# A delta-rule attention with two expert layers on one core: halves in turn, a shared copy, loads without padding

## The chip, the cores and the metric

The program runs on one core of a Trainium2 chip. Its time is the device time of one execution in microseconds (us), taken as the median of several runs on the chip. One execution was recorded by the hardware profiler; rows of that trace are quoted below.

A core has a matrix engine (PE; its weight loads are told apart as PEld), a vector engine (DVE), a scalar engine (ACT), a general engine (POOL) and an engine that here only issues transfers (SP). Each works through its own list of instructions in order, and they wait for one another by semaphores. PE reads from the on-chip memory SBUF and writes into PSUM, which DVE and ACT read back.

## The reference

Three layers follow one another. The first is a recurrence over 768 tokens for 4 batches of 8 heads with 48 features; the state of a head is a 48 by 48 matrix:

```python
for t in range(S):
    y[:, :, t] = np.einsum('bhd,bhde->bhe', q[:, :, t], state)
    v_old = np.einsum('bhde,bhd->bhe', state, kt)          # kt: normalised key
    state = state + bt[:, :, :, None] * np.einsum('bhd,bhe->bhde', kt, vt - v_old)
```

Its output, seen as 3072 tokens of 384 features, goes through two layers of the same shape, each a product with a 384 by 2048 matrix, a function of each element, and a product with a 2048 by 384 matrix:

```python
h = x @ w_in;  g = np.where(h > 0.0, h, np.exp(np.minimum(h, 0.0)) - 1.0);  x = g @ w_out
h = x @ w_in2; g = P(h) / (Q(h) + 1e-06);  out = g @ w_out2   # P cubic, Q from |h| and h*h
```

## The kernel before

**The recurrence in chunks.** The 768 tokens are cut into 12 chunks of 64 (s = 0 to 11), and two chunks make a window (six of them). Within a chunk the recurrence is a triangular system. The 32 heads lie as two halves of 16 (hf = 0, 1), each half in tiles of its own: 8 positions u by two blocks of partitions h. A half's tile of features has 64 partitions per block, of which 48 carry features; the other 16 hold zeros that `layout` (`rows`, L1653) puts there. No product reads them: the slices are `o:o + D` with D = 48.

For a window the gram products (`g_item`, L895, tiles gp) give all key-key and key-query products. From them DVE inverts the triangular systems in a row of some 60 small steps (`t_pieces`, L940), which ends in the tile tp_t. Then comes, for each chunk, a chain of small PE products with a copy or subtraction after each (`chain`, L1070): `ks` subtracts the old state's prediction (none for s = 0), `solve` (block 0), copy to ub, `lo`, subtract in R (for s = 0 in kv), `solve` (block 1), copy to ub, `yy` makes the outputs, `ku` the state update, `xx` transposes the outputs for the next layer. In `solve` and `lo` the loops run over u, then h, then hf, so that two PSUM tiles, one for each half, are filled in alternation, and both are complete only at the end.

The new state is taken out of PSUM in `ku`: one full tile for half 0, two tiles of 64 partitions for half 1. For s = 0 all three are copies by ACT (`move`, L1088), for later chunks three additions by DVE.

**The layers.** Wide groups of nine products of 128 by 512 (H into tiles h, O into tiles o) make the first expert layer, window by window, 16 H and 16 O groups each; the small groups of the next window's chain stand between them. The second expert layer (tiles h_a, h_b, o) follows without small groups. All weights pass a conversion on ACT and DVE first (raw, ce, wi, wo).

**Who sets the order.** The program is recorded first and then put in order by a planner (`order`, L355): it plays the recorded operations through a table of costs, gives each operation a latest start and repeats that for the eight entries of `PUSH` (L338), keeping the best. `MIX` (L330) is a list of pairs that breaks ties: each pair redraws a pseudo-random share of them. The planner's order is what each engine executes. Where it expects PE to idle before the first wide group, `gaps` (L397) puts in fillers, products whose result is not used (tile fill).

**Loads.** SP issues all transfers in one list. gin (xg and wo hold the first of them) are the gram inputs of a half chunk, kq the key-query tiles, kv keys and values. `gin_ahead` (L816) and `ch_ahead` (L842) issue each tile of gin and kq as one transfer of 128 partitions by 4 KB. Eight semaphores serve the transfers in turn, so one that would be the ninth in flight waits for the first. `hold` and `follow` (L717, L720) are copies of one column by POOL that keep a transfer back until something else is there; `follow` makes the second half's gin wait for the first half's.

Of the kernel before, what the change touches and what calls it, by code (L numbers as in the profile page):

```python
# [20 lines left out]
D = 48  # L21
NSC = 12
# [164 lines left out]
class Recorder:  # L187
# [62 lines left out]
    def mm(self, out, lhsT, rhs, start, stop):  # L250
        kind = self.group.kind
        pitch, lat = PEC[kind]
        self.add("PE", self.nc.tensor.matmul, dict(out=out, lhsT=lhsT, rhs=rhs, start=start, stop=stop), [out], [lhsT, rhs], pitch, lat)
# [74 lines left out]
SIZE = {"F": 9, "yy": 32, "yt": 48, "y2": 64}  # L328
SLACK = {"small": 150, "F": 100, "x": 30, "issue": 450, "rate": 385, "land": 2300, "wait": 900, "space": 3500, "room": 264, "first": 460, "blk": 253.9, "use": 2250, "hold": 400, "jit": 300, "keep": 6000, "most": 5000, "step": 3500, "drift": 0,  "pj": 0}
MIX = [  # L330
# [4 lines left out]
]  # L335


PUSH = [(16000, 5000), (5000, 3000), (16000, 3000), (0, 3000), (20000, 3000), (13000, 3000), (0, 500), (18000, 3000)]  # L338


def draw(seed, n):
# [282 lines left out]
def kernel(  # L624
# [93 lines left out]
        gpsimd.tensor_copy(out=t[:, 0, 0:1], in_=gate[-1])  # L718

    def follow(t, u):  # L720
        gpsimd.tensor_copy(out=t[:, 0, 0:1], in_=u[:, 0, 0:1])

    conv_q = []
    for f in range(NF):
# [91 lines left out]
    def gin_ahead(n):  # L816
        for _ in range(n):
            i = gin_n[0]
            if i == len(gin_q) or i >= 4 and len(gate) < 2:
                return  # L820
            park = i < 6
            if park or gin_l[0] < 2:
                w, s, hf = gin_q[i]
                if park:
                    t = gin_park(i)
                else:
                    t = ap2.tile([128, 1024], F32, tag="gin", name="gin", bufs=2)
                    gin_l[0] += 1
                t = t.rearrange("p (u n) -> p u n", u=8)
                if 4 <= i < 8:  # L830
                    hold(t)
                elif i >= 8 and hf:
                    follow(t, gin_t[s, 0][0])
                rc.dma(out=t, in_=c_kg[s, hf])
                gin_t[s, hf] = t, not park
                gin_n[0] += 1

# [4 lines left out]
    def ch_ahead(nm):  # L842
        if ch_n[nm] < len(ch_q):
            s, hf = ch_q[ch_n[nm]]
            if nm == "kq":
                t = ap2.tile([128, 8, 128], F32, tag="kq", name="kq")
                if s == 1:
                    hold(t)
                rc.dma(out=t, in_=c_kq[s, hf])
            else:  # L850
                if s == 1:
                    t = mp.tile([128, 2, DM], F32R, tag="wor", name="kv").bitcast(F32)
                    t = t.rearrange("p a b -> p (a b)").rearrange("p (u n) -> p u n", u=8)
                    hold(t)
                else:
                    t = ap2.tile([128, 8, 96], F32, tag="kv", name="kv")
                    if s == 0:
                        hold(t)
                rc.dma(out=t, in_=c_kv[s, hf])
            ch_t[nm, s, hf] = t  # L860
            ch_n[nm] += 1
# [11 lines left out]
    def cross(hf):  # L873
        if hf == 0:
            return [(slice(0, 128), slice(0, 128))]
        return [(slice(64 * h, 64 * h + 64), slice(64 - 64 * h, 128 - 64 * h)) for h in range(2)]

    def grp(h, blk, u):
        o = 64 * h + 32 * (blk ^ u % 2)
        return slice(o, o + 32)  # L880
# [189 lines left out]
    def chain(w, slots=SLOTS):  # L1070
# [14 lines left out]
        for j, s in enumerate(WINS[w]):  # L1085
# [38 lines left out]

            def solve(blk, s=s, st=st):
                rc.brk("s8" if s > 1 else "so")
                for u in range(8):
                    for h in range(2):
                        for hf, d in enumerate(st):
                            v = u ^ hf  # L1130
                            rs = grp(h, blk, v)
                            mm(out=d["cb"][over(s, hf, rs), v], lhsT=tp_t[rs, d["wu"] + v], rhs=d["R"][rs, v], start=True, stop=True)

            def u1(s=s, st=st, solve=solve):
                for d in st:
# [6 lines left out]

            def lo(j=j, s=s, st=st):
                rc.brk("l8" if s > 1 else "lo")
                for u in range(8):
                    for h in range(2):
                        for hf, d in enumerate(st):
                            v = u ^ hf
                            rs, os = grp(h, 0, v), grp(h, 1, v)
                            mm(out=d["cb"][over(s, hf, os), v], lhsT=gl_d[w][rs, d["wu"] + v, 32:64], rhs=d["ub"][rs, v], start=True, stop=True)  # L1150
                for hf, d in enumerate(st):
                    for o, c in cross(hf if s > 1 else 0):
                        vector.tensor_tensor(out=d["R"][o], in0=d["R"][o], in1=d["cb"][c], op=ALU.subtract)
# [57 lines left out]
            def ku(hf, s=s, st=st):  # L1211
                ps = [pa.tile([128, 8, D], F32, tag="pa", name="ku") for _ in range(2)]
                rc.brk("ku")
                for u in range(8):
                    for hf, d in enumerate(st):
                        for h in range(2):
                            rs, o = slice(64 * h, 64 * h + 64), 64 * (h ^ hf)
                            mm(out=ps[hf][o:o + D, u], lhsT=d["kv"][rs, u, 0:D], rhs=d["ub"][rs, u], start=True, stop=True)
                for hf in range(2):
                    for o, c in cross(hf):  # L1220
                        sl = s_st[o, 8 * hf:8 * hf + 8]
                        if s == 0:
                            move(sl, ps[hf][c], hf)
                        else:
                            vector.tensor_tensor(out=sl, in0=sl, in1=ps[hf][c], op=ALU.add)
                for _ in range(2):
                    ch_ahead("kv")
# [411 lines left out]
def layout(q, k, v, beta, moe_w_in, moe_w_out, moe2_w_in, moe2_w_out, moe2_a, moe2_b):  # L1639
    import numpy as np  # L1640

    f32 = np.float32
    B, H, S, Dh = q.shape

    def feat(x):
        t = x.reshape(B, 4, 2, NSC, 64, Dh)
        return t.transpose(3, 0, 2, 5, 1, 4).reshape(NSC, B, 96, 4, 64)

    def tok(x):
        t = x.reshape(B, 4, 2, NSC, 2, 32, Dh)  # L1650
        return t.transpose(3, 0, 2, 4, 5, 1, 6)

    def rows(k, q, cross):  # L1653
        kq = np.concatenate([k, q], axis=-1).reshape(NSC, 2, 2, 2, Dh, 4, 128)
        o = np.zeros((NSC, 2, 2, 64, 8, 128), f32)
        for hf in range(2):
            for h in range(2):
                o[:, hf, h ^ (hf * cross), :Dh] = kq[:, hf, :, h].transpose(0, 2, 1, 3, 4).reshape(NSC, Dh, 8, 128)
        return o.reshape(NSC, 2, 128, 8, 128)

    kf, qf = feat(k), feat(q)
    c_kg = rows(kf, qf, 1)
    kf = kf.copy()
    kf[:, :, :, 1::2] = np.roll(kf[:, :, :, 1::2], 32, axis=-1)
    c_kq = rows(kf, qf, 0)
    kt, vt = tok(k), tok(v)
    kv = np.concatenate([kt, vt], axis=-1)
    kv[..., 1::2, :] = kv[:, :, :, ::-1, :, 1::2].copy()
    c_kv = kv.reshape(NSC, 2, 2, 128, 4, 96).transpose(0, 1, 3, 2, 4, 5).reshape(NSC, 2, 128, 8, 96)
    bt = beta.reshape(B, 4, 2, NSC, 2, 32).transpose(3, 2, 4, 0, 1, 5).copy()  # L1670
    bt[:, :, :, :, 1::2] = bt[:, :, ::-1, :, 1::2].copy()
    bt = bt.reshape(NSC, 4, 16, 32)
    beta_l = np.concatenate([bt[0::2], bt[1::2]], axis=2)
    tk = np.arange(64)
    tpart = np.arange(128) % 64
    mask_p = np.concatenate(
        [(t[:, None] < tk[None, :]).astype(f32) for t in (tpart, (tpart + 32) % 64)] + [np.eye(128, dtype=f32)], axis=1)
    moe_w_in, moe_w_out, moe2_w_in, moe2_w_out = (
        w.view(np.int64) for w in (moe_w_in, moe_w_out, moe2_w_in, moe2_w_out))

    def w_in_tiles(w):
        return w.reshape(3, 128, NF, 128).transpose(2, 1, 0, 3).reshape(NF, 128, DM)

    d = {
        'c_kg': c_kg, 'c_kq': c_kq, 'c_kv': c_kv, 'beta_l': beta_l.reshape(len(WINS), 128, 32),
        'mask_p': mask_p,
        'w_in1': w_in_tiles(moe_w_in),
        'w_out1': moe_w_out.reshape(NF, 128, DM),
        'w_in2': w_in_tiles(moe2_w_in), 'w_out2': moe2_w_out.reshape(NF, 128, DM),
        'a_co': moe2_a, 'b_co': moe2_b,  # L1690
    }
    return {n: np.ascontiguousarray(x) for n, x in d.items()}
# [22 lines left out]
```

## Time and profile before

| | us |
|---|---|
| median of 3 runs | 966.79 |
| lowest, highest | 965.37, 967.17 |
| the profiled execution | 966.62 |
| its span, first to last instruction | 964.8 |
| PE busy in the span | 943.4 |
| first gram product | 6.87 |
| first `solve` product (chunk 0) | 45.50 |
| first wide group | 69.12 |
| last wide group's end, about | 960 |

The profiled execution took 966.62 us, of which 964.8 are the span of its trace. The stages of the span are: loads and gram products of window 0; the inversion on DVE, up to 45.50; the chain of the first two chunks, up to 69.12; and the stream of wide groups, in which PE is busy nearly all the time. A row of the timeline gives start, duration, engine, line, operation, output and inputs, and in brackets the idle time before it with what ended it. Line 206 is the helper that issues every recorded operation, so the tiles tell the rows apart.

### The profile page before, as it was taken

How to read it: one execution, taken by the hardware profiler on the slowest of the kernel's cores; microseconds unless marked ns; L12 is line 12 of the kernel's file. 1: busy time of each engine (PE TensorE's matmuls, PEld its weight loads, DVE VectorE, ACT ScalarE, POOL GpSimd, SP SyncE). 2: the span in 40 equal slices, each digit the busy share in tenths (PEclk: the TensorE clock that was granted, in tenths of full speed). 3: DMA queues.
4: the chain of work that ended last, by engine and by line, in shares of the span. 5: the costliest groups of instructions: out<-in, count | busy, mean ns of one | idle time of the engine just before them, and what ended most of it. 6: DMA issues, size and time to landing. Idle time of an engine off the chain costs nothing.

```text
span 964.8 us, 24786 instructions
## 1 busy us (share of the span) xinstructions
PE 943.4 (98%) x10312; PEld 752.8 (78%) x10312; DVE 832.5 (86%) x1182; ACT 693.3 (72%) x1311; POOL 312.8 (32%) x227
## 2 busy tenths in 40 slices
PE   8789999999999999999999999999999999999997
PEld 4367777877778878887888888888888888888885
DVE  5899999998999888975645369999999999999997
ACT  5387899777878778778866666776776766766764
POOL 2100002423312322222222244363544643743432
PEclk9799999999999999999999999999999999999999
DMA  8364545234544455344529321020010010000000
GB/s 297 138 195 129 191 129 178 87 99 152 190 136 153 152 150 178 102 134 139 177 88 393 133 73 43 1 66 1 1 66 0 14 54 1 33 1 0 34 1 33
DMA packets 59521, 99.89 MB, mean 104 GB/s; under 512 B 6544, under 2 KB 39440, under 8 KB 59408
## 3 DMA queue, kind: packets, MB, share of 16 engines
q1 hardware_dynamic: 59408, 98.30, 31.1%
q8 instruction: 81, 1.33, 0.6%
q14 instruction: 32, 0.26, 0.1%
HBM read 76.25 MB, written 22.02 MB: 102 GB/s over the span
## 4 chain that ended last, share of the span: by engine, by line
PE 80%; DMA 3%; ACT 2%; DVE 2%; issue 0%; POOL 0%; ACTq 0%; SPq 0%; DVEq 0%; POOLq 0%
PE o L206 37%; PE h L206 16%; PE h_b L206 11%; PE h_a L206 10%; PE pa L206 7%; PE h_c L206 1%; DMA raw<-w_out 1%; DMA wo<-w_out 1%; ACT wo L206 1%; DVE wo L206 1%; DMA kv<-c_kv 1%; DMA gin<-c_kg 0%; ACT e L206 0%; ACT raw L206 0%; DVE gh L206 0%
## 5 line engine op out<-in xcount | busy, mean ns | idle before, releaser
L206 POOL TENSOR_TENSOR gl<-wo 128x1024 fp32r<-128x1024 f32 (+1 forms) x48 | 145.9, 3040 | 205.1 <-DVE wo L206 130.5
L206 PE MATMUL o<-gh,wor 128*128 128x512 f32 x576 | 198.1, 399 | 0.1
L206 PE MATMUL h<-xh,wi 128*128 128x512 f32 x546 | 186.2, 397 | 0.3 <-DVE e L206 0.3
L206 ACT ACTIVATE wo<-wo 128x1024 f32<-128x1024 f32 (+3 forms) x202 | 134.4, 698 | 61.8 <-DVE wo L206 55.8
L206 POOL TENSOR_TENSOR wor<-wo,wor 128x384 fp32r<-128x384 f32 x80 | 87.9, 1100 | 250.0 <-ACT wor L206 233.7
L206 PE MATMUL o<-gh,wo 128*128 128x512 f32 x576 | 138.5, 389 | 0.0
L206 PEld LDWEIGHTS o<-gh,wor 128*128 128x128 f32 x576 | 107.9, 188 | 25.4 <-DVE wor L206 0.7
L206 PEld LDWEIGHTS o<-gh,wo 128*128 128x128 f32 x576 | 108.1, 188 | 22.5
L206 PEld LDWEIGHTS h<-xh,wi 128*128 128x128 f32 x546 | 102.4, 188 | 24.5 <-issue 1.3
L206 PE MATMUL o<-gl,wor 128*128 128x512 f32 x288 | 112.4, 390 | 0.0
L206 PE MATMUL h<-xl,wi 128*128 128x512 f32 x273 | 106.6, 390 | 0.1
L206 DVE TENSOR_TENSOR gl<-e,gh 128x512 fp32r<-128x512 f32 x88 | 77.2, 878 | 26.0 <-ACT gh L206 25.1
L206 PE MATMUL h_b<-xh,wi 128*128 128x512 f32 x300 | 96.4, 389 | 0.0
L206 DVE SCALAR_TENSOR_TENSOR e<-e,h 128x512 f32<-128x512 f32 x91 | 62.3, 685 | 35.6 <-ACT e L206 34.3
L206 DVE SCALAR_TENSOR_TENSOR wo<-wo 128x1024 f32<-128x1024 f32 (+2 forms) x71 | 80.5, 1138 | 10.2 <-ACT wo L206 10.1
L206 PE MATMUL h_a<-xh,wi 128*128 128x512 f32 x276 | 88.8, 389 | 0.0
L206 ACT ACTIVATE e<-h 128x512 f32<-128x512 f32 x91 | 54.2, 596 | 29.2 <-PE h L206 28.5
L206 PE MATMUL o<-gl,wo 128*128 128x512 f32 x288 | 73.5, 390 | 1.2 <-POOL gl L206 0.7
L206 DVE SCALAR_TENSOR_TENSOR gh<-wo,ab_sb 128x1024 fp32r<-128x1024 f32 (+1 forms) x49 | 65.1, 1329 | 9.1 <-ACT wo L206 3.1
L206 ACT ACTIVATE gh<-e 128x512 fp32r<-128x512 f32 x96 | 60.0, 625 | 13.7 <-DVE e L206 8.2
L206 ACT ACTIVATE wor<-wo 128x384 fp32r<-128x384 f32 x96 | 49.8, 520 | 26.5 <-PE o L206 25.0
L206 ACT ACTIVATE wo<-h_b,ab_sb 128x1024 f32<-128x1024 f32 (+1 forms) x52 | 57.2, 1128 | 15.8 <-PE h_b L206 12.7
(176 smaller groups left out, 1802.1 us busy)
## 6 DMA issues: line engine op xcount, KB each, us to landing
kq<-c_kq SPq DMA_DIRECT2D x22, 512.0 KB, 5.3
kv<-c_kv SPq DMA_DIRECT2D x24, 384.0 KB, 5.0
gin<-c_kg SPq DMA_DIRECT2D x18, 512.0 KB, 4.0
raw<-w_out SPq DMA_DIRECT2D x42, 192.0 KB, 2.7
raw<-w_in SPq DMA_DIRECT2D x34, 192.0 KB, 3.1
o2d<-cs SPq DMA_DIRECT2D x32, 192.0 KB, 2.9
i2d<-cs SPq DMA_DIRECT2D x32, 192.0 KB, 2.5
wi<-i2d SPq DMA_DIRECT2D x16, 384.0 KB, 4.4
```

Of the source, the lines that this page charges most:

```text
L206: fn(**{k: v.real() if isinstance(v, View) else v for k, v in kw.items()})
```

## The change

Four things are edited, and the planner's tables with them.

1. `solve` and `lo` take their order from a new function `turns`. For s = 0 and 1 it runs over hf first, then u and h: half 0's sixteen products, then half 1's. For later chunks the order is as before.
2. In `ku` for s = 0 the two copies of half 1 go to DVE; half 0's copy stays on ACT.
3. The tiles of gin and kq are loaded as two transfers of 48 partitions each, without the zero rows; the arrays in main memory lose these rows. `follow` makes two copies of one column, one for each block of 48.
4. `MIX` has 5 entries instead of 23 and `PUSH` other values, so the planner orders the whole program anew.

```diff
 MIX = [
-    (12345, 1), (56619490, 20), (79100030, 20), (98034153, 200), (72433589, 200), (58365895, 600),
...
+    (12345, 1), (81752085, 20), (3694915, 60), (24019981, 60), (78021846, 200),
 ]
-PUSH = [(16000, 5000), (5000, 3000), (16000, 3000), (0, 3000), (20000, 3000), (13000, 3000), (0, 500), (18000, 3000)]
+PUSH = [(14000, 2000), (10000, 0), (21000, 0), (0, 0), (23000, 0), (11000, 0), (2000, 0), (20000, 5000)]
...
     def follow(t, u):
-        gpsimd.tensor_copy(out=t[:, 0, 0:1], in_=u[:, 0, 0:1])
+        for h in range(2):
+            r = slice(64 * h, 64 * h + D)
+            gpsimd.tensor_copy(out=t[r, 0, 0:1], in_=u[r, 0, 0:1])
...
-                rc.dma(out=t, in_=c_kg[s, hf])
+                for h in range(2):
+                    rc.dma(out=t[64 * h:64 * h + D], in_=c_kg[s, hf, h])
...
-                rc.dma(out=t, in_=c_kq[s, hf])
+                for h in range(2):
+                    rc.dma(out=t[64 * h:64 * h + D], in_=c_kq[s, hf, h])
...
+    def turns(s):
+        if s > 1:
+            return [(hf, u, h) for u in range(8) for h in range(2) for hf in range(2)]
+        return [(hf, u, h) for hf in range(2) for u in range(8) for h in range(2)]
...
             def solve(blk, s=s, st=st):
                 rc.brk("s8" if s > 1 else "so")
-                for u in range(8):
-                    for h in range(2):
-                        for hf, d in enumerate(st):
-                            v = u ^ hf
-                            rs = grp(h, blk, v)
-                            mm(out=d["cb"][over(s, hf, rs), v], lhsT=tp_t[rs, d["wu"] + v], rhs=d["R"][rs, v], start=True, stop=True)
+                for hf, u, h in turns(s):
+                    d, v = st[hf], u ^ hf
+                    rs = grp(h, blk, v)
+                    mm(out=d["cb"][over(s, hf, rs), v], lhsT=tp_t[rs, d["wu"] + v], rhs=d["R"][rs, v], start=True, stop=True)
...
                         sl = s_st[o, 8 * hf:8 * hf + 8]
-                        if s == 0:
+                        if s == 0 and hf:
+                            vector.tensor_copy(out=sl, in_=ps[hf][c])
+                        elif s == 0:
                             move(sl, ps[hf][c], hf)
```

On PE, the chain of chunk 0 begins as follows before. Tile pa_81 is half 0's PSUM tile, pa_82 half 1's; tp_t is the inverse, ub the copied solution, gl the gram tile, and fill a filler.

```order
L1629 MATMUL fill<-tt,cm_sb 128x256
L206 MATMUL pa_81<-kv,tp_t 32x48
L206 MATMUL pa_82<-kv,tp_t 32x48
...
L1629 MATMUL fill<-cm_sb 128x256
L206 MATMUL pa_81<-ub,gl__175 32x48
L206 MATMUL pa_82<-ub,gl__175 32x48
...
```

The same place of the changed kernel:

```order
L1633 MATMUL fill<-tt,cm_sb 128x256
L206 MATMUL pa_81<-kv,tp_t 32x48 x16
L206 MATMUL pa_82<-kv,tp_t 32x48 x16
L206 MATMUL pa_81<-ub,gl__179 32x48 x16
L206 MATMUL pa_82<-ub,gl__179 32x48 x16
L206 MATMUL pa_81<-kv,tp_t 32x48 x16
L206 MATMUL pa_82<-kv,tp_t 32x48 x16
L206 MATMUL h_148<-ub,p 64x48
```

Sixteen products of one half now stand together, and the fillers between these three groups are gone; between the first `solve` and the first wide group there are five fillers instead of seven.

On DVE, the subtraction of chunk 0 (kv) and the two state copies (s_st) stand among steps for window 1 (am, x, nb, rr), conversions (ce, wi, wo) and masks (p). In the changed kernel:

```order
L206 TENSOR_TENSOR kv<-kv,pa_81 128x8x48
L206 TENSOR_TENSOR kv<-kv,pa_82 128x8x48
L206 TENSOR_TENSOR wi_329<-ce,wi_329 128x192 x2
L206 TENSOR_SCALAR x<-am 128x32
L206 SCALAR_TENSOR_TENSOR ce<-wo_91 128x192
L206 TENSOR_SCALAR t_721<-x 128x32
L206 SCALAR_TENSOR_TENSOR ce<-wo_91 128x192
L206 SCALAR_TENSOR_TENSOR wo_91<-wo_91 128x192
...
L206 TENSOR_TENSOR p<-p,cm_sb 128x256
L206 RECIPROCAL x<-x 128x32
L206 COPY s_st<-pa_81 64x384 x2
```

Before, no copy of the state stands on DVE; the same place reads:

```order
L206 TENSOR_TENSOR kv<-kv,pa_81 128x8x48
L206 TENSOR_TENSOR kv<-kv,pa_82 128x8x48
L206 TENSOR_SCALAR t_681<-x 128x32
L206 TENSOR_TENSOR nb<-rr,x 128x32
L206 SCALAR_TENSOR_TENSOR ce<-wo_91 128x192
L206 SCALAR_TENSOR_TENSOR x<-nb,t_681 128x32
```

Thirteen operations now stand between the subtraction and the two copies. In the stream of wide groups the changed kernel has the same products and, as before, 77 stretches of small products between the wide groups; which small group stands in which stretch differs in many places.

## Rows read from the trace of the kernel before

**Rows 1.** The page, part 1: busy time, share and instructions of each engine.

```profile
PE 943.4 (98%) x10312; PEld 752.8 (78%) x10312; DVE 832.5 (86%) x1182; ACT 693.3 (72%) x1311; POOL 312.8 (32%) x227
```

**Rows 2.** Windows by stage: busy of PE, PEld, DVE, ACT, POOL; clock, DMA, GB/s.

```profile
13.34:45.50 32.16, 25.89 (x300) 12.29 (x299) 29.39 (x54) 15.06 (x54) 5.62 (x14) 0.84 0.56 201
45.50:69.12 23.62, 20.15 (x795) 14.39 (x795) 20.72 (x67) 18.76 (x64) 1.93 (x3) 1.00 0.59 186
69.12:147.00 77.88, 76.09 (x1338) 59.45 (x1337) 74.41 (x176) 66.47 (x180) 2.55 (x5) 1.00 0.48 153
```

**Rows 3.** Waits of PE from 69.2 to 946 us: total, times, longest.

```profile
PE pa L206 <- DVE R L206: 1.3, 5, 0.3
PE pa L206 <- ACT ub L206: 0.6, 1, 0.6
```

**Rows 4.** Timeline of the gram stage, PE: start, duration, idle before.

```profile
1.45 5.49 PE L206 MATMUL pa<-tmp 128*128 128x512 f32 x6 [1.45 <-DVE tmp L288]
...
6.87 1.02 PE L206 MATMUL pa<-wo 48*32 48x128 f32 x61
...
9.49 0.30 PE L206 MATMUL gp<-xg 48*32 48x128 f32 x2 [0.38 <-DMA xg<-c_kg]
...
12.48 0.24 PE L206 MATMUL pa<-wo 48*32 48x64 f32 x2 [1.45 <-issue]
```

**Rows 5.** DMA view of four stretches: queue of instructions (packets, MB, share).

```profile
q8 instruction: 6, 0.10, 1.7%
q8 instruction: 1, 0.02, 32.3%
q8 instruction: 1, 0.02, 41.5%
q8 instruction: 1, 0.02, 32.6%
```

**Rows 6.** The page, part 3: the same queue over the whole span.

```profile
q8 instruction: 81, 1.33, 0.6%
```

**Rows 7.** Timeline before the first solve: filler and transposition.

```profile
39.56 6.02 PE L1629 MATMUL fill<-tt,cm_sb 128*128 128x512 f32 x13
...
42.54 1.97 DVE L206 STREAM_TRANSPOSE tp_t<-am 128x1024 f32<-128x1024 f32 x1
```

**Rows 8.** Windows before the first solve; the eighth column is the granted clock.

```profile
35.13:40.96 5.83, 5.83 (x7) 2.49 (x8) 5.17 (x7) 0.00 (x0) 0.00 (x0) 0.50 0.26 91
```

**Rows 9.** Timeline of the chain of chunk 0.

```profile
45.50 0.88 PE L206 MATMUL pa<-kv,tp_t 32*32 32x48 f32 x64
...
46.44 0.87 ACT L206 ACTIVATE ub<-pa 128x384 f32<-128x384 f32 x2 [1.35 <-PE pa L206]
...
48.47 1.02 DVE L206 TENSOR_TENSOR kv<-kv,pa 128x384 f32<-128x384 f32 x2 [1.05 <-PE pa L206]
...
50.48 0.87 ACT L206 ACTIVATE ub<-pa 128x384 f32<-128x384 f32 x2
...
52.46 1.50 ACT L206 ACTIVATE s_st<-pa 128x384 f32<-128x384 f32 x3
...
53.07 0.66 PE L206 MATMUL y<-ub,p 64*64 64x48 f32 x26 [0.54 <-issue]
...
54.14 1.15 PE L206 MATMUL pa<-s_st,kq 48*64 48x48 f32 x64
```

**Rows 10.** Timeline of PE at the end of the chain of chunk 1.

```profile
65.44 0.27 PE L206 MATMUL y<-s_st,kq 48*64 48x48 f32 x5 [1.45 <-issue]
...
69.12 0.51 PE L206 MATMUL h<-xh,wi 128*128 128x512 f32 x1
```

**Rows 11.** The page, part 6: issues, KB each, median us to landing.

```profile
gin<-c_kg SPq DMA_DIRECT2D x18, 512.0 KB, 4.0
raw<-w_out SPq DMA_DIRECT2D x42, 192.0 KB, 2.7
```

**Rows 12.** Waits of the queue that issues transfers, whole span.

```profile
SPq L206 <- DVE ce L206: 113.6, 46, 13.6
```

More of the change, by code (lines that the diff above doesn't have):

```diff
@@ L1144, in lo @@
                 rc.brk("l8" if s > 1 else "lo")
[L1145 to L1150, printed above, removed]
+                for hf, u, h in turns(s):
+                    d, v = st[hf], u ^ hf
+                    rs, os = grp(h, 0, v), grp(h, 1, v)
+                    mm(out=d["cb"][over(s, hf, os), v], lhsT=gl_d[w][rs, d["wu"] + v, 32:64], rhs=d["ub"][rs, v], start=True, stop=True)
                 for hf, d in enumerate(st):
@@ L1654, in rows @@
         kq = np.concatenate([k, q], axis=-1).reshape(NSC, 2, 2, 2, Dh, 4, 128)
-        o = np.zeros((NSC, 2, 2, 64, 8, 128), f32)
+        o = np.zeros((NSC, 2, 2, Dh, 8, 128), f32)
         for hf in range(2):
             for h in range(2):
-                o[:, hf, h ^ (hf * cross), :Dh] = kq[:, hf, :, h].transpose(0, 2, 1, 3, 4).reshape(NSC, Dh, 8, 128)
-        return o.reshape(NSC, 2, 128, 8, 128)
+                o[:, hf, h ^ (hf * cross)] = kq[:, hf, :, h].transpose(0, 2, 1, 3, 4).reshape(NSC, Dh, 8, 128)
+        return o
     kf, qf = feat(k), feat(q)
```

3 rows, old and new, of the table MIX are left out of this document.

## The prediction

> **What bounds the kernel now.** I read the page first, then the windows by stage, the waits of PE, and last the timeline of the first 70 us. The reader should see on the page that PE is busy 98% of the span [rows 1]. Between 69.2 and 946 us its two largest waits, 1.3 and 0.6 us, are for R and ub [rows 3]: in the stream of wide groups there are some 2 us to be had and no more. Both kernels have the same products there and 77 stretches of small products between wide groups, so the number of changes between the two kinds is equal. What the edits can move lies before 69.12: the gram products from 6.87 on [rows 4], 32.16 us of inversion up to 45.50, and 23.62 us of chain for chunks 0 and 1 [rows 2]. Each microsecond taken from there starts the stream earlier, since the first wide group needs both chunks' outputs.
>
> In the chain PE does not wait for data alone. Two of its waits are put down to "issue", nothing that the profile shows: 0.54 us at 53.07 and 1.45 us at 65.44 [rows 9, 10]; a third one of 1.45 us stands in the last gram group at 12.48 [rows 4]. I read these as PE out of instructions. The queue of instructions moved 81 packets and 1.33 MB, 16.4 KB each [rows 6]; PE ran 10,312 products and as many loads [rows 1], 255 instructions per packet. A packet lies 2.5 to 2.7 us ahead of the restart at 12.48 and 2.8 to 3.0 us ahead of that at 65.44 [rows 4, 5, 10]. The chain has 795 product and 795 load records [rows 2], 6.2 packets' worth, and six packets came in it [rows 5]: one per 3.9 us. A full step of 64 products with their loads takes 0.88 us [rows 9], so PE could use up a packet in 1.8 us. The supply is not far from being the chain's bound already.
>
> **The change part by part.** The sum is made against the profiled execution, 966.62 us: a span of 964.8 and 1.8 around it. The median of the runs shown is 966.79, 0.17 more.
>
> *Loads without zero rows.* 46 transfers of 512 KB (24 of gin, 22 of kq) become 92 of 192 KB. In the gram stage the first product starts at 6.87, when the warm-up products end (1.45 + 5.49 = 6.94) [rows 4], so the first two tiles are already there and a faster load of them gains nothing. The fourth tile costs 0.38 us at 9.49 [rows 4]; with a quarter fewer bytes ahead of it that goes. What is late next is the instruction packet: the last gram group stops at 11.0 and goes on at 12.48. Fewer bytes in flight at 8 to 10 us may let the packet through sooner. Gain 0 to 1.2 us; I take 0.4, near the wait that surely goes, because the packet's 2.6 us from view to use remain.
>
> [...] No run here shows a transfer of 48 partitions yet. [...]
>
> The row nearest to a new transfer is raw<-w_out: 192 KB land 2.7 us after issue, against 4.0 for gin's 512 KB [rows 11]. The 46 added issues fall on SP, whose list waits for others' data most of the time (113.6 us for ce alone) [rows 12]; that cover is gone only where a load is issued just before its use, as in the gram stage, where the last of the four gin tiles is the eighth and ninth issue instead of the fifth. If that made the fourth tile late instead of early, it would cost about 1 us, and this is the lower end for the term.
>
> `follow`: one more copy of a column for each of eight tiles, on POOL, which is busy 32% of the span [rows 1]. Nothing.
>
> *Filler before the first solve.* The inverse tp_t is ready at 42.54 + 1.97 = 44.51, but the filler runs until 39.56 + 6.02 = 45.58, and the first solve starts at 45.50 [rows 7, 9]. Here PE is 1.0 us late by itself. [...] Bounds: 0.2 lost and 1.0 gained; I take 0.4, the middle.
>
> *Halves in turn.* Before, a step is 64 products of alternating halves (0.88), then two copies (0.87) or two subtractions (1.02), and the next step's products can run through only after the second of these [rows 9]: about 1.9 us per step. In turn, the first half is done after 0.44, its copy takes 0.44 beside the second half's products, and the next step's first half can start about 1.05 us after the last. Each chunk has two such transitions inside (solve to lo, lo to solve), 0.85 us each, and one at its end that must wait for both halves (0.44). Twice that is 4.3 us. *The state by two engines:* three copies in 1.50 us on ACT [rows 9] become one of 0.50 beside two on DVE of about 0.5 each, a gain of 0.5. It hangs on DVE being free: 13 operations stand ahead of the copies behind kv, each 0.1 to 0.35 us apart, some 3 us, and with the shorter chain they end just about when `ku` does. If they are late, the 0.5 is lost. Together 4.8 us if nothing else holds PE.
>
> But the same number of packets must come through: the chain has two fillers less out of some 1,600 instructions. A shorter dependency chain reaches the end of each packet earlier and waits there. What it keeps is only what earlier asking brings. Bounds: 4.8 us gained (packets never late) and 3.0 us lost (second rival). I take 1.0 gained, near the row of the 1.45 us wait: with a supply of one packet per 3.9 us and six packets, most of the gain turns into longer waits of the same kind at 49, 53, 57 and 65 us.
>
> *The new order of everything else.* Same products, same number of changes. At most 2 us of waits can go [rows 3], and about as much can come. 0.
>
> Sum: 966.62 - 0.4 - 0.4 - 1.0 = 964.8.
>
> **The rivals.** *Supply never in the way.* The chain then gains its full 4.8 us: 966.62 - 0.8 - 4.8 = 961.0. For it: only two of PE's waits in the chain are put down to issue [rows 9, 10], and there are fewer bytes on the DMA engines that carry the packets. Against it: the three waits above, all in dense small products. [...] Chance 0.13.
>
> *Supply falls behind: slower.* The place is the chain of chunk 1. After PE has run dry at 65.44, the next packet is seen only at 67.8 [rows 5, 10], 5.4 us after the one of 62.4, against 3.9 on average. If running dry makes the following packet late, the changed chain, which runs dry earlier, pays 1.5 us for each of two more packets: 3.0 us. With the 0.4 of the gram stage and no gain from the filler: 966.62 - 0.4 + 3.0 = 969.2. It decides from the second dry stop on. Chance 0.17.
>
> *The gain is waited out later.* In the first window DVE is busy 74.41 of 77.88 us, more than ACT [rows 2]. If DVE's work up to the end of that window sets its length, an earlier first wide group only waits longer for R, e or gl, and the time is 966.6: no change. For it: DVE's share; against it: PE waits hardly at all there [rows 3]. Also here falls the case in which the new order brings as many waits as the chain saves. Chance 0.25.
>
> **How the numbers follow.** The forecast, 964.8, has chance 0.45 and a range of its own from 963.4 to 966.2. A difference of 0.2%, 1.9 us, is about what a measurement of this kernel can tell from none, so faster means below 964.9 and slower above 968.7. Faster: the first rival's 0.13, a little over half of the forecast (0.27) and some of the third (0.06), 0.46. Slower: most of the second rival's, 0.15, and a little of the third. The rest, 0.38, is the same. The range from 961.5 to 968.6 leaves out the far end of the first rival and half of the second.
>
> **What would show it.** In the changed profile: no wait for xg near 9.5 and an "issue" wait in the last gram group of 1.5 us or less; the first solve 0.4 to 1.4 us before 45.50; in the chain ub copies of one half beside products of the other, and state copies on DVE; "issue" waits that add up to more than the 2.0 us of before; first wide group at 67.3, and the same distance as now from there to the end. The forecast is wrong if the chain shrinks by over 3 us or grows, or if PE's waits between first wide group and end differ by over 1.5 us from now.

## The result and the profile after

The changed kernel takes 977.59 us (median of 4, 977.27 to 978.30) against 966.93 us (median of 4, 965.37 to 967.17): a ratio of 1.0115, with an interval from 1.0097 to 1.0132. It is 10.7 us slower; 964.8 was forecast, with a range up to 968.6. The profiled spans are 976.5 and 964.8 us, 11.7 apart, and this difference can be followed step by step. (In the experiments below, one execution of p11, 1045.97 us at a granted clock of 0.847, is left out as one in a slower state.)

First the gram stage, from PE's timeline (columns as in [rows 4]):

```profile
6.87 1.41 PE L206 MATMUL pa<-wo 48*32 48x128 f32 x63
...
9.77 0.40 PE L206 MATMUL gp<-wo 48*32 48x128 f32 x2 [0.29 <-DMA wo<-c_kg]
...
11.71 0.30 PE L206 MATMUL gp<-xg 48*32 48x128 f32 x2 [1.54 <-DMA xg<-c_kg]
...
14.66 0.32 PE L206 MATMUL pa<-wo 48*32 48x64 f32 x2 [1.41 <-issue]
```

The first product still starts at 6.87, but the fourth tile, which cost 0.38 us of waiting at 9.49 [rows 4], now comes at 11.71 after a wait of 1.54, and the last group goes on at 14.66 in place of 12.48.

Then the inversion, the last filler and the chain of both chunks, PE again, with the transposition on DVE that makes tp_t:

```profile
37.84 0.42 PE L206 MATMUL pa<-gin 48*32 48x64 f32 x3 [4.10 <-issue]
...
42.55 7.57 PE L1633 MATMUL fill<-tt,cm_sb 128*128 128x512 f32 x18
50.05 0.88 PE L206 MATMUL pa<-kv,tp_t 32*32 32x48 f32 x64
...
54.03 0.50 PE L206 MATMUL pa<-kv,tp_t 32*32 32x48 f32 x26 [0.69 <-issue]
...
58.03 0.83 PE L206 MATMUL y<-ub,p 64*64 64x48 f32 x26 [1.83 <-issue]
58.79 2.07 PE L1633 MATMUL fill<-cm_sb 128*128 128x512 f32 x2
60.79 1.52 PE L206 MATMUL pa<-s_st,kq 48*64 48x48 f32 x64
...
70.86 0.27 PE L206 MATMUL y<-s_st,kq 48*64 48x48 f32 x4 [1.29 <-issue]
...
71.58 1.12 PE L1633 MATMUL fill<-cm_sb 128*128 128x512 f32 x2
...
74.96 0.51 PE L206 MATMUL h<-xh,wi 128*128 128x512 f32 x1
```

```profile
46.43 2.00 DVE L206 STREAM_TRANSPOSE tp_t<-am 128x1024 f32<-128x1024 f32 x1
```

A wait put down to "issue" has grown to 4.10 us at 37.84. tp_t is ready at 48.43 (before: 44.51 [rows 7]), the filler ends at 50.12, and the first solve starts at 50.05 in place of 45.50. In the chain the issue waits add up to 0.69 + 1.83 + 1.29 = 3.81 us (before: 1.99 [rows 9, 10]). The windows by stage, which answer to [rows 2]:

```profile
15.86:50.05 34.19, 29.33 (x305) 13.81 (x305) 30.38 (x53) 15.00 (x54) 5.07 (x15) 0.88 0.68 154
50.05:74.96 24.91, 19.59 (x791) 14.57 (x791) 19.07 (x62) 16.40 (x56) 0.31 (x1) 0.93 0.48 142
74.96:147.00 72.04, 67.06 (x1115) 51.37 (x1115) 66.48 (x144) 58.44 (x159) 6.42 (x9) 1.00 0.52 141
```

The chain takes 24.91 us in place of 23.62. The issue waits are not all of this. Right after the one of 1.83 us the granted clock falls to 0.50, the lower of the two levels in the profiles of before and after (0.50 and 1.00), for 3.4 us, where it was 1.00 throughout the chain before [rows 2]:

```profile
58.25:61.66 3.41, 3.41 (x59) 1.81 (x55) 1.03 (x7) 1.57 (x6) 0.00 (x0) 0.50 0.80 276
```

The filler in it takes 2.07 us, the same two products at 71.58 take 1.12; the 64 products with s_st take 1.52 instead of 1.15 and the 26 with p 0.83 instead of 0.66 [rows 9]. An estimate from these rows: 1.8 us more of issue waits and 1.5 of lower clock, less some 1.9 for the two fillers that are gone, make the chain's 1.3.

In the first window of the stream PE idles for 72.04 - 67.06 = 5.0 us, where it idled for 77.88 - 76.09 = 1.8; over the same 1507 products from the first wide one on it is 5.0 against 1.9. PE's waits from 75 us on, the answer to [rows 3]:

```profile
PE pa L206 <- ACT ub L206: 1.3, 2, 0.7
PE pa L206 <- ACT gl__1264 L206: 1.2, 1, 1.2
PE h L206 <- DVE wi L206: 1.1, 1, 1.1
PE h L206 <- DVE e L206: 0.9, 1, 0.9
```

The two profiles side by side, in us:

| stretch | before | after | longer by |
|---|---|---|---|
| to the first inversion step on DVE | 13.34 | 15.86 | 2.5 |
| inversion, to tp_t ready | 31.17 | 32.57 | 1.4 |
| tp_t to the first solve | 0.99 | 1.62 | 0.6 |
| chain of chunks 0 and 1 | 23.62 | 24.91 | 1.3 |
| first wide group to the end | 895.68 | 901.54 | 5.9 |

Of the products with wi, the 720th (495.03 us before, 506.80 after) and every later one lie 11.77 us late: from there on nothing differs.

### The profile page after: what moved, and what is told of

The parts are those of the page before. It is cut to its first block, busy times and chain, and to the rows that moved or that the text cites. A ratio compares the mean times of both kernels' runs of the same rounds, so it can differ in the third digit from the quotient of the medians.

```text
span 976.5 us, 24872 instructions
## 1 busy us (share of the span) xinstructions
PE 949.3 (97%) x10312; PEld 755.8 (77%) x10312; DVE 835.6 (86%) x1184; ACT 692.3 (71%) x1309; POOL 316.8 (32%) x235
## 4 chain that ended last, share of the span: by engine, by line
PE 83%; DVE 6%; DMA 4%; ACT 4%; issue 3%; POOL 0%; SPq 0%; ACTq 0%; DVEq 0%; POOLq 0%
PE o L206 37%; PE h L206 16%; PE h_b L206 10%; PE h_a L206 10%; PE pa L206 8%; PE fill L1633 1%; DMA kq<-c_kq 1%; PE h_c L206 1%; DVE wo L206 1%; DMA wo<-w_out 1%; DMA gin<-c_kg 1%; ACT e L206 1%; ACT wo L206 1%; DVE R L206 1%; DVE tmp L206 1%
## 5 line engine op out<-in xcount | busy, mean ns | idle before, releaser
L206 ACT ACTIVATE gh<-e 128x512 fp32r<-128x512 f32 x96 | 59.8, 623 | 11.7 <-DVE e L206 7.0
```

What stands on the lines that cost most here:

```text
L206: fn(**{k: v.real() if isinstance(v, View) else v for k, v in kw.items()})
```

## Experiments

A kernel of this program is planned anew after every edit, so an edit alone also moves thousands of other instructions. In most experiments the list of instructions was therefore kept: the planner saw the old operations, and only what was sent out in their place differs. A single profile is one execution; the unchanged kernel's runs spread from 964.6 to 970.7 us. Distances below are between medians, to the unchanged kernel measured beside each experiment; the intervals come from the single runs, and their middle need not be the ratio of the medians.

| kernel | order | us | against before | interval of the ratio |
|---|---|---|---|---|
| p1, full loads, copies late | after | 974.03 | +7.1 | 1.0062 to 1.0102 |
| p2, 48-row loads | before | 969.61 | +2.7 | 1.0021 to 1.0044 |
| p3, 64-row halves | before | 977.54 | +10.6 | 1.0094 to 1.0129 |
| p4, halves in turn | before | 968.08 | +1.2 | 0.9997 to 1.0023 |
| p5, full loads | after | 971.73 | +5.7 | 1.0040 to 1.0074 |
| p6, full loads, alternating | after | 971.47 | +5.4 | 1.0043 to 1.0069 |
| p7, even and odd rows | before | 972.02 | +6.0 | 1.0039 to 1.0078 |
| p8, cut fillers | before | 970.05 | +4.0 | 1.0026 to 1.0065 |
| p9, work left to the stream | before | 971.36 | +4.5 | 1.0028 to 1.0059 |
| e2, chain edits alone | new | 978.57 | +11.7 | 1.0088 to 1.0129 |
| e4, tables alone | new | 970.35 | +3.5 | 1.0022 to 1.0047 |
| e5, all edits, old tables | new | 982.46 | +15.6 | 1.0138 to 1.0196 |
| p10, 48 rows early | before | 969.56 | +2.0 | 1.0006 to 1.0037 |
| p11, 48 rows late | before | 967.92 | +0.4 | 1.0009 to 1.0032 |
| p12, work pulled ahead | before | 969.12 | +1.6 | 1.0007 to 1.0035 |

**Loads, p1, p2, p3.** The load is put in place of the planned one:

```diff
 p1, p5 (order of after)              p2 (order of before); p3 with 64 for 48
-dma(t[64h:64h+48], c[s,hf,h]) x2    -dma(t, c[s,hf])
+dma(t, c[s,hf])                     +dma(t[64h:64h+48], c[s,hf,h]) x2
```

> The changed kernel with its list of instructions kept, but each pair of 48-row loads is one 512 KB load of 128 rows again, issued where the first of the pair stood. Theory 1 (the 48-row loads are slow per byte and delay what shares the DMA engines with them): the gram stage ends 2 us sooner (last gram product resumes near 12.5 in place of 14.66), the issue wait of 4.10 us at 37.84 falls below 2, the first solve starts near 46 in place of 50.05, and the time falls by 4 to 5 us to about 973. Rival (the new order of everything else costs the 11 us): the time stays within 1 us of 977.6 and the first solve starts after 49. Rival (the chain's products by halves cost it): the same, with the chain as long as now (24.9 us).

> The kernel before with its list of instructions kept, but each 512 KB load of gin and kq tiles is two 192 KB loads of 48 rows in the same place. Theory 1 (48-row loads are slow): first solve at about 49.5 in place of 45.50, time about 971 (plus 4 to 5 us), with a DMA share of about 1 but under 200 GB/s in the first 25 us. Rival (fewer bytes cost nothing, the order does): within 1 us of 966.9.

> The kernel before with its list of instructions kept, but each 512 KB load is two 256 KB loads of 64 rows, zero rows with them. If it is the half of the partitions in one transfer that is slow, this is at least as slow as the 48-row version: 971 to 973, first solve at 50 or later. If only the issue of a second transfer cost time, it is as slow as the 48-row version. If it is the count of 48 rows (a bad split over the engines) that is slow, it stays within 1 us of 966.9.

In p1 the column copy that holds back a tile's second half ran behind the load and overwrote one column of it, so part of its gram products come from wrong values; p5 mends that, and only p5 is used below. p2: the 48-row loads alone cost 2.7 us; the first solve starts at 46.36, not at the 49.5 expected, since the gram stage's last group is only 1.4 us later (13.87) and the 1.0 us by which PE was late there before takes part of it. p3 costs 10.6 us, more than expected: dropping the zero rows does help, but not as much as halving the transfer hurts. In its profile 4.1 us of this stand before the first wide product (73.22) and 6.5 in the stream. What the halves do is in the windows of 0 to 6.87 us (the last two columns are the busy share of the DMA engines and GB/s), of before, after, p3 and p2 in this order:

```profile
0.00:6.87 6.87, 5.42 (x7) 1.85 (x7) 0.48 (x1) 1.59 (x2) 1.64 (x5) 1.00 0.74 247
```

```profile
0.00:6.87 6.87, 5.42 (x7) 1.85 (x7) 0.48 (x1) 1.28 (x1) 1.64 (x5) 1.00 0.78 146
```

```profile
0.00:6.87 6.87, 5.15 (x10) 1.99 (x10) 0.48 (x1) 1.28 (x1) 1.64 (x5) 1.00 0.69 168
```

```profile
0.00:6.87 6.87, 4.75 (x14) 1.87 (x14) 0.48 (x1) 1.28 (x1) 1.63 (x5) 1.00 0.77 174
```

The engines are about as busy as before and move 146, 168 and 174 GB/s instead of 247. Per busy share that is 187, 243 and 226 against 334. A tile of 48 rows twice has 25% fewer bytes than before, moved at 56% (after) or 68% (p2) of the rate, and so takes 1.1 to 1.3 times as long; this is an estimate, as other transfers share the window.

**Why halves are slow, p7.** Same count of transfers, rows and bytes as p3, other rows:

```diff
-dma(t[64*h:64*h+64], c[s,hf][64*h:64*h+64]) x2
+dma(t[h::2], c[s,hf][h::2]) x2
```

> The kernel before, its list of instructions kept, each 512 KB load as two of 64 rows, but one takes the even rows of the tile and the other the odd ones. If a transfer is slow because it goes to one half of the partitions, these two run as fast as the one of 128 rows: time 966.9 to 968.5, 350 GB/s or more in the gram stage. If a transfer of 64 rows or the second issue is slow in itself, it takes as long as two contiguous halves: 977.

```profile
0.00:6.87 6.87, 5.42 (x6) 1.86 (x7) 0.48 (x1) 1.28 (x1) 1.64 (x5) 1.00 0.60 192
```

Now 0.60 busy share moves 192 GB/s, 320 per busy share, nearly the 334 of whole tiles. So it is the contiguous half, and not the count or size of the pieces, that makes the engines slow. (The rows read from main memory change along with the partitions written; no run separates the two.) The time, +6.0, is neither of the two expected: 4.6 us of the 10.6 come back, the rest does not. Part of the rest is the second issue. SP issues the fourth gin tile, of before, after and p7 in this order, at

```profile
2.59 0.43 SPq L206 DMA_DIRECT2D xg<-c_kg  x1
```

```profile
3.98 0.89 SPq L206 DMA_DIRECT2D xg<-c_kg  x2
```

```profile
5.04 1.24 SPq L822 DMA_DIRECT2D xg<-c_kg  x2
```

and p7's PE waits for it longer than before (0.38 at 9.49 [rows 4]):

```profile
10.93 0.30 PE L206 MATMUL gp<-xg 48*32 48x128 f32 x2 [1.10 <-DMA xg<-c_kg]
```

That is the start alone: p7's first wide product (70.33) is 1.2 us late, and the 3.7 us more by which its profile is longer lie in the stream, where no run shows their cause. What makes a contiguous half slow, at 243 per busy share against 320 for even and odd rows, which reach both halves, and 334 for whole tiles, no run shows.

**Where the loads' price falls, p10 and p11** (48-row loads for the twelve tiles used ahead of the stream, or for all others):

> The kernel before, its list of instructions kept; two 48-row loads in place of one of 512 KB only for the tiles that are used ahead of the stream (the eight gram tiles of windows 0 and 1, the kq tiles of chunks 0 and 1). All tiles so loaded cost 2.7 us. If the price lies at the start, where PE waits for these loads and for packets behind them, this takes 968.5 to 970; if it lies in the stream, 966.5 to 967.5.

> The other way round: 48-row loads for all later tiles, 512 KB loads for the first twelve. Start theory: within 1 us of before, 966 to 968. Stream theory: 968.5 to 970. The two prices should add up to some 2.7 us.

The medians are 2.0 and 0.4 us away and would put the price at the start, but the intervals are nearly the same (0.6 to 3.6 and 0.9 to 3.1 us), so that the two cannot be told apart; that they add up to nearly p2's 2.7 may be luck. In the profiles the first wide product is 1.5, 1.4 and 2.5 us late in p2, p10 and p11, and the stream 2.7, 0.4 and 0.2 longer, which does not settle it either. In p10's first stage the waits of after are back, that for a packet too:

```profile
33.28 0.21 PE L206 MATMUL pa<-gin 48*32 48x64 f32 x1 [3.57 <-issue]
```

**Halves in turn, p4 and p6.**

```diff
 p4: the chain's products of before, sent out in another order
-for u: for h: for hf: product(hf, u, h)
+for hf: for u: for h: product(hf, u, h)
 p6: p5 with the reverse of this edit
```

> The kernel before with its list of instructions kept, but in the first two chunks the solve products come by halves (first half, then second). Theory 1 (instruction packets bound the chain): the chain from first solve to first wide group stays within 1 us of 23.6, its issue waits grow above 2.0 us, time 966 to 968. Rival (products and copies bound it): the chain loses 2 to 4 us, time 963 to 965. Rival (running dry earlier makes later packets late): the chain grows by over 1 us, time above 968.

> The first such run again with one thing mended: the column copies that hold a load back stand ahead of the whole 512 KB load, all of them, so that none runs behind it. So: the changed kernel's list of instructions, gin and kq loaded by one transfer of 128 rows each. If the loads are most of the loss (4 us in the kernel before by two 48-row loads in its own order: 2.7), the time is 973 to 974.5. If the pool copy that waited was what slowed the first version, it is 970 to 972.

> As the run before this one, and the solve products of the first two chunks alternate between the halves again: what is left of the change is the new order of everything else and the state copies. If the instruction packets bound the chain, this takes off 0 to 2 us (halves in turn cost 1.2 in the old order) and 971 to 974 is left, 4 to 7 above before, which is the price of the new order. If the new order costs nothing, it comes to 967 to 968.

p4's chain, from 45.68 to 71.24, takes 25.56 us instead of 23.62, and these are its stops:

```profile
53.17 0.66 PE L206 MATMUL y<-ub,p 64*64 64x48 f32 x26 [1.25 <-issue]
...
58.35 0.61 PE L206 MATMUL pa<-R,tp_t 32*32 32x48 f32 x36 [1.17 <-issue]
...
62.35 0.63 PE L206 MATMUL pa<-R,tp_t 32*32 32x48 f32 x40 [0.26 <-issue]
...
66.36 0.27 PE L206 MATMUL y<-s_st,kq 48*64 48x48 f32 x5 [1.95 <-issue]
```

1.25 + 1.17 + 0.26 + 1.95 = 4.63 us in place of 1.99, while PE's waits for data in the chain fall from 1.1 to 0.6 us. Again the granted clock is at its lower level for a while, after the last stop:

```profile
67.87:71.28 3.41, 3.41 (x73) 2.52 (x71) 1.58 (x4) 2.01 (x5) 0.00 (x0) 0.50 0.91 337
```

From that stop's end to the first wide product p4 takes 4.88 us (66.36 to 71.24), before 3.68 (65.44 to 69.12): 1.2 of the chain's 1.9 us stand here, with the same products. The median of p4 says +1.2, within the interval of no change. In the order of after, the edit is worth nothing either (p5 less p6: 0.3, with intervals that overlap). Over all profiles, the six kernels with halves in turn have chains of 24.5 to 26.8 us, the eleven others 23.6 to 27.5. As the clock fell within the chain in six of them (after, p4, p5, p6, e5, p12), these lengths compare only roughly.

That these are instruction packets can be read off PE's records. Numbering products, weight loads and PE's few semaphore instructions in order of start, the stops end at these records, give or take two:

| kernel | first record behind each "issue" wait |
|---|---|
| before | 448, 960, 1728, 2496 |
| after | 448, 960, 1472, 1728, 2496 |
| p4 | 448, 960, 1728, 1984, 2240, 2496 |
| p6 | 448, 960, 1728 |
| e2 | 448, 960, 1472, 1728, 1984, 2240, 2496 |

Each is 192 + 256 n, in kernels whose products there differ, and so is every other one in the seventeen profiles: every 256th instruction, beside the 255 per packet of 16.4 KB by [rows 1, 6]. Where one border after the other is a stop, they lie 4.0 to 5.2 us apart (p4, above), and the stretch from record 1728 to record 2496 takes 12.4 us in before, 12.8 in after, 13.2 in p4. In these dense small products the stops cost 0.2 to 5.3 us each.

**More instructions, p8** (each filler in the chain cut into products of 64 columns):

```diff
-matmul(w[:, 0:256n], c, v broadcast to 256n columns)
+for a in range(0, 256n, 64): matmul(w[:, a:a+64], c, v[:, 0:64])
```

> The kernel before, but each filler between first solve and first wide group is cut into products of 64 columns: the same columns, some 200 instructions more in the chain, none of which anything waits for. If packets of 256 instructions bound the chain, it grows by about 3 us (0.8 packets at 3.9 us), less what the present slack takes, with all waits put down to issue beginning at records 448, 960, 1472, 1728, 1984, 2240, 2496 of PE as in all kernels so far: time 968.5 to 970. If the products and copies bound it, the time changes only by what the fillers themselves get longer (under 1 us): 966.5 to 967.9.

Inconclusive on the time: +4.0, but a cut filler itself takes longer than its columns did, 2.00 us for 1.12 at one place and 4.7 us in all seven, so both theories allow it. In its profile (966.74 us, its fastest execution) the first wide product comes 2.8 us late and the 720th with wi 0.1: there a later start of the stream was made up for. The stops do move to other products and stay at 256 n + 192 (1728, 2240, 2752):

```profile
47.28 2.00 PE L1631 MATMUL fill<-cm_sb 128*128 128x64 f32 x16
...
61.54 0.37 PE L206 MATMUL pa<-ub,gl__175 32*32 32x48 f32 x14 [0.89 <-issue]
```

**The new order, p9, e2, e4, e5.** p5 and p6 leave 5.4 to 5.7 us that neither loads nor halves explain. Busy time and count of DVE and ACT (they stand behind PE and PEld) up to the first wide group, and from there to the last product with wi, of before, then of after:

```profile
0.00:69.12 69.12, 56.10 (x1356) 32.56 (x1357) 52.85 (x127) 38.24 (x128) 10.43 (x32) 0.93 0.63 212
69.12:945.80 876.68, 874.05 (x8902) 710.24 (x8902) 767.15 (x1040) 647.80 (x1172) 298.39 (x193) 1.00 0.30 96
```

```profile
0.00:74.96 74.96, 60.09 (x1356) 34.80 (x1357) 52.19 (x121) 35.90 (x120) 8.26 (x31) 0.91 0.67 164
74.96:957.60 882.64, 875.93 (x8902) 711.01 (x8902) 770.94 (x1048) 649.10 (x1178) 304.55 (x202) 1.00 0.30 91
```

The new order does 121 and 120 operations ahead of the stream where before did 127 and 128: of the inversion of window 1 and of the weights' conversion fewer steps stand there (two of DVE's 121 are the state copies, which ACT did before). By these rows PE waits 6.71 us in the stream instead of 2.63, 4.1 of the 6.0 us that it is longer; it is also busy 1.9 us longer, and no row gives the cause of that. DVE has 770.94 us to do in the stream in place of 767.15; 1.3 of these 3.8 us fall ahead of the 145th product with wi, about the window that it filled to 95% before [rows 2]. p9 does this to the order of before: 7 such steps on DVE and 7 on ACT, and a load that waits for one of them, are sent out behind the first wide group.

```diff
+late = last 5 inversion steps and 2 conversions on DVE, 6 conversions and 1 step on ACT
+first[:end] = [o for o in first[:end] if o not in late] + late
```

> The kernel before, its list of instructions kept, but the last preparatory steps that stand before the first wide group on DVE (5 steps of window 1's inversion, 2 of the weights' conversion) and on ACT (6 of conversion, 1 of the inversion) are put right behind it, as many as the changed kernel's order has there. If the work that the new order leaves to the first window of the stream is what makes its stream 4 to 5 us longer, the distance from the first wide group to the end grows by 2.5 to 5 us (DVE has some 3 us more to do in a window that it fills to 95%) and the time is 968.5 to 971. Rival (other places of the new order cost it): the distance grows by under 1 us, time 966 to 967.5.

```profile
70.43 0.62 PE L206 MATMUL h<-xh,wi 128*128 128x512 f32 x2
...
78.00 0.50 PE L206 MATMUL h<-xh,wi 128*128 128x512 f32 x1 [2.56 <-DVE e L206]
...
78.57 1.04 PE L206 MATMUL h<-xh,wi 128*128 128x512 f32 x2
```

```profile
78.57:81.98 3.41, 3.41 (x28) 2.27 (x34) 3.10 (x5) 2.95 (x7) 0.00 (x0) 0.50 0.00 0
```

+4.5 us, and in the profile the lateness grows from 0.4 us at the first wide product to 4.7 at the 48th (3.7 remain at the end), behind one wait for e of 2.56 us and, right after it, 3.4 us at the lower clock, in which the same pair of products takes 1.04 us instead of 0.62. That so much work left to the stream costs some 4.5 us (2.7 to 5.7 by the interval), the lower clock included, is shown; that it is all that the new order costs is not: in after, p5 and p6 the waits stand at other products (wi 1.1, gl 1.2 to 1.3). p6's profile has the lower clock in three stretches (60.99 to 64.41, 98.54 to 101.95, 108.78 to 112.19), before none between 40.96 and 962 us; how much of p6's 5.4 us that makes is not separated.

> Products by halves and the state copies alone, with 512 KB loads and the planner's tables of before; the planner makes a new order for it. If any new order costs what the changed kernel's costs (its lists were fitted to other code), 970 to 973. If only the changed kernel's tables are unlucky and the chain's edits cost 1 us, 967 to 968.5. If the chain's edits gain as I predicted, 965 to 966.

> The code of before with the planner's tables of the changed kernel: another order of the same instructions, nothing else. If an order drawn by other tables costs 4 to 5 us by itself, 970 to 972. If the order costs only where it was made for a chain thought shorter, 966 to 968.

> The changed code, all edits in, with the planner's tables of before. If the 48-row loads (3 to 6 us) and a new order (4 to 5 us) add up whatever the tables, 974 to 978. If the changed kernel's tables are at fault, loads and chain edits alone: 969.5 to 971.5.

Every other order that the planner drew is slower than that of before: tables alone +3.5 us, as the first expectation said, chain edits alone under the old tables +11.7 and all edits under the old tables +15.6, both more than any of theirs. So the tables of after are not unlucky; they save 4.9 us against the old ones on the same code. Of these orders that of before is the exceptional one.

**Work pulled ahead, p12:** four conversions on ACT put in front of the last copies of y, into ACT's idle time.

```diff
+first = first[:seat] + four conversions + rest
```

> The kernel before with four conversions on ACT (1.4 us) taken from behind the first wide group to the place ahead of the last copy of y, where ACT idles for 1.3 us because PE has no instructions. If what is prepared ahead of the stream shortens its first window, as work left to it lengthens it, 965 to 966.5. If ACT's part of that work is not what the stream waits for (its waits are for DVE), 966.5 to 967.5.

+1.6 us, above both expectations. The idle time is no room for them, since their weights are not there yet, and the granted clock falls as well, for the end of the chain and the first wide products:

```profile
64.87 0.66 ACT L206 ACTIVATE wo<-wo 128x192 f32<-128x192 f32 x2 [0.51 <-DMA wo<-w_out]
67.66 0.64 ACT L206 ACTIVATE wo<-wo 128x192 f32<-128x192 f32 x2 [2.13 <-DMA wo<-w_in]
```

```profile
66.68:73.51 6.83, 6.22 (x76) 4.54 (x76) 4.32 (x9) 4.81 (x14) 0.00 (x0) 0.50 0.53 182
```

No kernel here beats the one before.

## Why the prediction was wrong

**The bound.** That packets limit the chain was right, and the evidence is now better than the 3.9 us per packet that I worked with: stops at every 256th record. What I drew from it was not. Two signs of a wrong forecast that it named came: the chain grew, and PE's waits behind the first wide group rose by 4.1 us. Its premise that each microsecond gained ahead of the stream starts the stream earlier is not all of the time either: p8's lost 2.8 us were made up for, and p6, whose stream starts 0.1 us earlier than before, takes 5.4 us more.

**Loads, -0.4: wrong in sign, and with the new order one of the two largest misses.** "With a quarter fewer bytes ahead of it that goes" counted bytes. The rate per busy share fell to between 56 and 68%. In the order of before that costs 2.7 us (p2), in that of after 977.59 - 966.93 less 971.73 - 966.06, 5.0 us (with 2.4 either way by the two intervals, so the two prices are not clearly different). The lower end, "about 1 us" for a late fourth tile, was the right event (a wait of 1.54 for xg). Its cause there, the issue on SP, can have a part in it: SP is done with that tile at 4.87 instead of 3.02, and p7, at nearly the full rate, waits 1.10 too. How the 2.2 us by which the tile's products are late (11.71 against 9.49) divide between issue and rate is open. The raw<-w_out row, 192 KB in 2.7 us [rows 11], was no model: its rows fill 128 partitions. That a transfer to a contiguous half is itself slow had no place in the term; two of them in place of one of the whole tile, with the same bytes, cost 10.6 us in p3.

**Filler, -0.4:** no run shows this term, the middle of 0.2 lost and 1.0 gained. The gram stage brought nothing that could be passed on, and in after PE is late by 1.6 us there instead of 1.0. The last 18 products of filler ran at a granted clock of 1.00 throughout, in 7.57 us, where the filler of before spent its first 5.83 us at 0.50 [rows 8]; but they start at 42.55 instead of 35.13, behind the wait of 4.10 us at 37.84.

**Halves in turn and state copies, -1.0: measured +1.2 in the order of before, 0.3 in that of after, neither clear of noise.** "What it keeps is only what earlier asking brings" was the failed step: asking earlier brings nothing, as the packets come at their own pace (12.4 to 13.2 us from record 1728 to 2496, above). This is near the second rival's mechanism (waits of 4.63 us in p4, two dry stops more), at less than half of its 3.0 us; but 1.2 of the 1.9 us of p4's chain stand at the lower clock, a term that neither the sum nor a rival had for the chain. The state copies on their own were not run; they are within p6's 5.4.

**New order, 0 with 2 either way: measured 3.5 (e4, another new order) to 5.4 (p6).** The reasoning, same products and same number of changes, is true of after. But it looked at PE alone. Work for DVE and ACT that stood beside the chain now stands in the stream, which by itself costs 4.5 us in p9; for after itself this cause is argued. The third rival named the place (DVE's share in the first window [rows 2]) but allowed no loss there: it took the work in that window as fixed.

**The sum.** Loads 5.0, new order with the state copies 5.4, halves 0.3: 10.7, the difference measured. This adds up by construction, as after, p5 and p6 are one series of edits; with the pieces priced in the order of before (2.7, 4.5, 1.2) it is 8.4, and 2.3 us are left, within what the intervals allow or due to how they act together, for instance slow loads under a shorter chain. That is open.

## What to carry to other kernels

Before splitting a transfer to drop bytes, ask which partitions each piece reaches: per busy share, contiguous halves here moved 187 to 243 GB/s where whole tiles moved 334 (56 to 73%), and even and odd rows 320 (96%). Where an engine runs thousands of tiny instructions, number its records: here the stops stood 256 records apart or a multiple of it, beside 255 instructions per packet, and reordering the steps brought nothing (p4 +1.2 us; p5 less p6 0.3). Before a stretch's length is put down to a wait, look at its granted clock: in after a wait of 1.83 us was followed by 3.4 us at a granted clock of 0.50, in p9 one of 2.56 us by the same. And where a planner places work, an edit's price includes the order drawn for it: keep the list and change only what is sent out, or the edit is not what is measured.

## What the hardware showed unexpectedly

One stop was longer where contiguous halves were in flight. The stop at record 960 costs 1.68 us in before (at 29.14), 1.69 in p5 and 1.92 in p7, and 0.8 to 2.4 in the twelve kernels without contiguous halves at the start, but 4.10 in after, 4.61 in p2, 3.56 in p3 and 3.57 in p10, where contiguous halves are in flight; e5, the fifth with them, stops at record 704 instead, for 5.29. That the data delay the packets is read from these rows; no run varied it by itself.

The granted clock fell in mid-program. In after, p4, p5, p9 and p12 it fell to 0.50 between 0.2 and 1.7 us after PE had waited for 1.7 to 2.6 us in one piece, and stayed there for 3.4 to 6.8 us; but p11 waited for 2.20 us up to 54.44 and kept 1.00 through its chain, so that such a wait alone does not decide it. No run varied this by itself either.
